# Head outputs to token rows: a 64-column weight block for the 64-token tile, and fixed PSUM banks

## The chip, the cores and the metric

One core of a Trainium2 chip runs the whole program. The metric is the device time of one execution in microseconds. The kernel before was run three times: 501.88, 502.3 and 503.22 us, median 502.3 us. Lower is better.

## The reference

Two batches, 8 heads, 576 tokens, head dimension 64. Queries and keys are rotated, then come softmax attention, the gathering of the heads into rows of 512 numbers a token (1152 tokens), a routed layer with 8 experts, of which each token takes one, and a last gated layer:

```python
scores = scale * np.matmul(q_rot, k_rot.transpose(0, 1, 3, 2))
attn = np.exp(scores - max) ; attn = attn / (sum + 1e-09)
x = (attn @ v).transpose(0, 2, 1, 3).reshape(B * S, H * D)        # token rows
logits = x @ w_gate + modality_bias[modality_id]                  # chooses the expert
out[mask] = gate_w[mask, None] * (np.maximum(x[mask] @ w1[e], 0) @ w2[e])
h = out @ w_in ; result = (h * np.tanh(softplus(h))) @ w_out
```

All in float32.

## The kernel before, in words

**Stages.** Attention (about 17 to 170 us), then expert tiles of 304 token rows with weights that are chosen at run time (to about 291 us), then the last gated layer. Products that need more than one pass of the tensor engine's number format are done with a high and a low part (`F32R` tiles named `..h` and `..l`); the transposes and the products that make token rows are plain float32.

**Attention by units.** 576 queries of a head fall into tiles of 128, 128, 64, 128, 128 (`QT`). The 64-query tile of two neighbouring heads is worked as one shared tile (`QMIX`, j = 2): rows 0 to 63 for the odd head, 64 to 127 for the even one. Each head has two units (`Unit`): hf = 0 with the tiles up to 320 queries, hf = 1 with the last two. A unit goes through these steps, each by its own function:

- `score` (PE, L963), `smax` (DVE, L973), `sexp` (ACT, L984): scores in PSUM, the negated row maximum, the exponentials. For the shared tile the scores of the odd head's queries take a 128-column and those of the even head's a 64-column weight operand.
- `tr` (PE, L997): exponentials are transposed, 128 or, for the last key block, 64 keys at a time, into a PSUM bank.
- `t_hi` (ACT, L1017) and `t_lo` (DVE, L1023): high and low part of the bank into SBUF. After `t_lo` the bank is free.
- `pv` (PE, L1038): the product with the values, accumulated in the bank `avp`, head dimension on the partitions (high part 0 to 63, low part 64 to 127), queries along the row; `f_evac` (ACT, L1047) copies it to `avt`.
- `f_mm` (PE, L1068): turns the head output round into token rows. The weight operand is a block of 128 columns of `avt` (128 queries), the moving operand `mov` has 72 columns: an identity that adds high and low part, and the head's 8 columns of the routing weights. A unit hf = 1 has two blocks; a unit hf = 0 has three, the third being the 64-query tile. For even heads the third block starts at column 256, its last 64 columns being a stretch of `avt` set to zero at the start; for odd heads it starts at column 0, and its last 64 columns are queries of the next tile. The three blocks lie side by side in one PSUM bank.
- `f_norm` (DVE, L1078): multiplies all 128 rows of the two or three blocks by the reciprocal sums and writes token rows `X`. Rows 64 to 127 of the 64-query tile's block are no token's, and no later step takes them as one.

**Banks.** Three PSUM banks `pt0` to `pt2` serve `tr`, `f_mm` and the routing's `counts` in turn. `bank` makes a new tile under the tag of the bank whose turn it is; the tile framework adds the waits on the readers of the tile that stood there before.

**Order.** `Plan` writes the order of all instructions of the stage ahead of time: a greedy list over PE, ACT, DVE, POOL and the SP queue. Each step has an assumed duration, dependences, resources that it takes and gives back (bank ring, exponentials, score banks) and a due time (`K`, 10 units a head). At each turn the step that can start earliest is issued; among those that can start at once the one due first. Some steps may go to one of two engines. An engine's clock in the plan goes on by the assumed duration. The routing of the first batch (L337 to L524), its scatters on POOL (L408) and the first expert tile's preparation are worked in as streams, once their conditions are met. The listing of `f_mm` (L1179) is `0.22 * len(u.cols)`, so 0.44 or 0.66.

**After attention.** Expert weights are loaded by the SP queue in chunks (`wraw`) as their buffers come free, after the routing table is in registers; the last layer's packed weights (`wr`) are loaded in between and unpacked on DVE.

Of the kernel before, what the change touches and what calls it, by code (L numbers as in the profile page):

```python
# [10 lines left out]
F32 = mybir.dt.float32  # L11
# [7 lines left out]
B, H, S, D = 2, 8, 576, 64  # L19
# [193 lines left out]
def moe_kernel(ctx: ExitStack, tc: tile.TileContext, aps, out):  # L213
# [596 lines left out]
    def attention(actx, hook):  # L810
# [5 lines left out]
        ps_t = actx.enter_context(tc.tile_pool(name="ps_t", bufs=1, space=PSUM))  # L816

        avp = ps_t.tile([128, 512], F32, tag="av", name="av")
        scp = [ps_s.tile([128, 2, 512], F32, tag=f"sc{z}", name=f"sc{z}") for z in range(2)]
        cur["rtile"] = scp[0][:, 1, NC2:512]  # L820
        spare = [0, 0.0, 0]
# [13 lines left out]
        mov = a_c.tile([128, H, XW], F32, name="mov")  # L835
# [10 lines left out]
                )  # L846

        def bank(name):
            return ps_t.tile([128, 512], F32, tag=f"pt{plan.at}", name=name)

        vraw, vhl, xin, ab, qk = {}, {}, {}, {}, {}
        sc, pexp, st, rs, pt, ph, pl, av, avsb, xo, nm = ({} for _ in range(11))
# [137 lines left out]
        def tr(n, hf, kts):  # L990
            kn = KT[kts[0]][1]
            pt[n, hf, kts] = t = bank(f"pt{n}_{hf}_{kts[0]}")
            o = 0
            for kt in kts:
                k0 = KT[kt][0]
                for j in U[n, hf].js:
                    nc.tensor.transpose(  # L997
                        out=t[:kn, o:o + 128], in_=pexp[n, j][:, k0:k0 + kn], identity=ident
                    )
                    o += 128  # L1000
# [63 lines left out]
        def f_mm(n, hf):  # L1064
            t = bank(f"xo{n}_{hf}")
            xo[n, hf] = t[:, :3 * XW].rearrange("p (a c) -> p a c", a=3)
            for i, c in enumerate(U[n, hf].cols):
                nc.tensor.matmul(  # L1068
                    xo[n, hf][:, i], lhsT=avsb[n, hf][:, c:c + 128], rhs=mov[:, n % H],
                    start=True, stop=True,  # L1070
                )

        def f_norm(n, hf):
# [20 lines left out]
        plan = Plan(  # L1094
            {"pe": 9.6, "act": 11.0, "dve": 11.8, "pool": 10.0, "sp": 7.0},
            {"sc": [0.0] * 2, "pexp": [0.0] * 5, "ph": [0.0] * 2, "pha": [0.0], "av": [0.0], "qs": [0.0, 8.6],
             "vhl": [0.0] * 2, "xs": [], "vraw": [11.9], "ab": [0.0], "avt0": [0.0],
             "avt1": [0.0], "st": [0.0] * 8},
            [0.0] * 3,
        )  # L1100
# [4 lines left out]
        def op(name, eng, dur, key, fn, *a, deps=(), line=None, **kw):  # L1105
            go = (lambda: fn(*a)) if isinstance(eng, str) else lambda: fn(*a, plan.eng)
            plan.op((name,) + a, eng, dur, key, go, deps=deps, line=line, **kw)

        for n in range(B * H):
            z = 10.0 * n  # L1110
# [20 lines left out]
        for q in range(4 * (B * H) // 2):  # L1131
            p, o = divmod(q, 4)
            n, hf = 2 * p + ORDER[o][0], ORDER[o][1]
            z = 20.0 * p
            if o == 0:
                tiles = groups = 0
            u = U[n, hf]
            for i, j in enumerate(u.js):
                k = tiles + i
                line = [("score",) + was] * bool(was)  # L1140
                op("score", "pe", 0.525 if j == QMIX else 0.485, z + K["sc"][k], score, n, j,
                   deps=[("stack", n)] + [("stack", n + 1)] * (j == QMIX) + line,
                   take=[("sc", (n, j))], give=[("qs", n)] * (j == QMIX or (n % 2 and j == 4)))
                op("max", "dve", 0.665, z + K["max"][k], smax, n, j, deps=[("score", n, j)])
                line = [("exp",) + e_was] * bool(was)
                op("exp", "act", 0.717, z + K["exp"][k], sexp, n, hf, i, j,
                   deps=[("max", n, j)] + line,
                   take=[("pexp", 0)] + ([("st", (n, hf))] if i == 0 else []),
                   give=[("sc", (n, j))])
                was, e_was = (n, j), (n, hf, i, j)  # L1150
            last = len(u.groups) - 1
            pair = "pha" if u.pair else "ph"
            for i, kts in enumerate(u.groups):
                m = len(kts)
                a = (n, hf, kts)
                k = groups + i
                prev = (n, hf, u.groups[i - 1])
                op("tr", "pe", 0.11 * m * len(u.js), z + K["tr"][k], tr, *a,
                   deps=[("exp", n, hf, x, j) for x, j in enumerate(u.js)],
                   take=[("ring", a)], give=[("pexp", 0)] * len(u.js) if i == last else [],  # L1160
                   line="tr")
                op("hi", "act", 0.05 + u.w * m / 1200.0, z + K["hi"][k], t_hi, *a,
                   deps=[("tr",) + a] + [("hi",) + prev] * (i > 0),
                   take=[(pair, a)] if i == 0 and o != 2 else [], line="hi")
                op("lo", "dve", 0.07 + u.w * m / 960.0, z + K["lo"][k], t_lo, *a,
                   deps=[("hi",) + a], give=[("ring", a)], line="lo")
                more = [("lo", n - 1, 0, (kt,)) for kt in kts] if o == 2 else []
                op("pv", "pe", u.nq * m / 2400.0 * (1 if i == last else 2), z + K["pv"][k], pv, *a,
                   deps=[("lo",) + a, ("vlo", n)] + [("pv",) + prev] * (i > 0) + more,
                   take=[("av", a)] if i == 0 else [], line="pv",  # L1170
                   give=([(pair, a)] * (o != 1) + [("vhl", n)] * (o % 2)) * (i == last))
            a = (n, hf)
            op("evac", "act", 0.05 + u.nq / 1200.0, z + K["evac"][o], f_evac, *a,
               deps=[("pv", n, hf, u.groups[-1])], take=[(f"avt{hf}", a)], give=[("av", a)])
            op("rec", "pool", 0.2 if o == 2 else 0.1, z + K["rec"][o], f_rec, *a,
               deps=[("exp", n, hf, len(u.js) - 1, u.js[-1])],
               give=[("st", a)] * ((1, 0, 2, 1)[o]))
            op("inv", "dve", 0.09, z + K["norm"][o] - 2.0, f_inv, *a, deps=[("rec",) + a])
            op("fmm", "pe", 0.22 * len(u.cols), z + K["fmm"][o], f_mm, *a, deps=[("evac",) + a],  # L1179
               take=[("ring", a)], give=[(f"avt{hf}", a)])  # L1180
            op("norm", "dve", 0.08 + 0.095 * len(u.cols), z + K["norm"][o], f_norm, *a,
               deps=[("fmm",) + a, ("inv",) + a], give=[("ring", a)])
            tiles += len(u.js)
            groups += len(u.groups)
        for i in range(14):
            op("zero", "sp", 0.5, 20.0 + 5.0 * i, setup_dma, i, deps=[("stack", 3 + i // 3)])
        op("bias", "pool", 2.5, 60.0, setup_bias)
        hook(plan, bank)
        plan.run()

# [83 lines left out]
    with ExitStack() as actx:  # L1274
        attention(actx, hook)
# [63 lines left out]
    with ExitStack() as mctx:  # L1339
# [87 lines left out]
        def pool(name, bufs, **kw):  # L1427
            return ectx.enter_context(
                tc.tile_pool(name=name, bufs=bufs, reuse_waits="tile", **kw)
            )  # L1430

        w2p, yp, gp, op = (
            pool(n, b) for n, b in (("w2p", 1), ("yp", 1), ("gp", 3), ("op", 5))
        )
# [129 lines left out]
        for q in range(nq):  # L1564
# [9 lines left out]
            for i in range(2):  # L1574
                u = LATE.get((nq - q, i), m + i)
# [6 lines left out]
            o = m + Q["o"]  # L1582
# [14 lines left out]
        for i, (q, t) in enumerate(TAIL):  # L1597
            w = 2 * nq + (0.6 if i < 5 else 4)
# [75 lines left out]
```

## Time and profile before

| | us |
|---|---|
| median of three runs | 502.3 |
| profiled execution | 500.64 |
| its span, first to last instruction | 498.9 |
| PE busy | 469.3 |
| DVE busy | 397.7 |
| POOL busy | 362.8 |
| ACT busy | 331.4 |

Busy time is the union of the instructions of an engine. Matmuls are pipelined and their ends are modelled, so overlapping ones count once, and a busy PE need not be at its peak. PEld is the engine's weight load, PEldq its queue's separate semaphore instructions. The chain of waits is followed back from the last instruction; its pieces give start and length in microseconds, the engine, the kernel line and the number of instructions. The granted TensorE clock was 0.999 of full speed over the whole span, 2.4 GHz.

### The profile page before, as it was taken

How to read it: one execution, taken by the hardware profiler on the slowest of the kernel's cores; microseconds unless marked ns; L12 is line 12 of the kernel's file. 1: busy time of each engine (PE TensorE's matmuls, PEld its weight loads, DVE VectorE, ACT ScalarE, POOL GpSimd, SP SyncE). 2: the span in 40 equal slices, each digit the busy share in tenths (PEclk: the TensorE clock that was granted, in tenths of full speed). 3: DMA queues.
4: the chain of work that ended last, by engine and by line, in shares of the span. 5: the costliest groups of instructions: out<-in, count | busy, mean ns of one | idle time of the engine just before them, and what ended most of it. 6: DMA issues, size and time to landing. Idle time of an engine off the chain costs nothing.

```text
span 498.9 us, 9097 instructions
## 1 busy us (share of the span) xinstructions
PE 469.3 (94%) x3152; PEld 436.9 (88%) x3152; DVE 397.7 (80%) x614; ACT 331.4 (66%) x750; POOL 362.8 (73%) x367
## 2 busy tenths in 40 slices
PE   0689999998999999999999999999999999999995
PEld 0589999998998798998989998899889989999994
DVE  5878989899788676663586879999999958777773
ACT  2378888777776845554465488665755878767763
POOL 4979999999970455765767567778777769966764
PEclk9999999999999999999999999999999999999999
DMA  7579995787654278895888630020100001100002
GB/s 220 131 180 218 242 232 169 186 211 190 161 157 166 84 224 333 324 313 211 284 301 315 235 107 0 2 85 11 76 0 1 1 1 62 44 1 1 3 1 84
DMA packets 24132, 69.43 MB, mean 139 GB/s; under 512 B 5522, under 2 KB 9810, under 8 KB 22034
## 3 DMA queue, kind: packets, MB, share of 16 engines
q1 hardware_dynamic: 21794, 63.16, 41.5%
q0 software_dynamic: 1456, 5.03, 2.5%
q10 hardware_dynamic: 832, 0.61, 0.5%
q8 instruction: 26, 0.43, 0.3%
q14 instruction: 24, 0.20, 0.1%
HBM read 49.08 MB, written 6.44 MB: 111 GB/s over the span
## 4 chain that ended last, share of the span: by engine, by line
PE 68%; DVE 15%; issue 5%; DMA 4%; ACT 4%; POOL 3%; POOLq 0%; SPq 0%; ACTq 0%; DVEq 0%
PE h L1471 15%; PE o L1528 14%; PE mm L695 13%; PE sc L963 8%; PE av L1038 7%; PE pt L997 7%; DVE ta L1493 6%; PE xo L1068 3%; DVE nm L973 2%; DMA wr<-in_wio_dram 1%; DMA tabs<-in_rope_dram 1%; DMA wraw(0, 1)_6_3129<-in_w_dram 1%; PE mm L661 1%; DVE pl L1023 1%; ACT pexp L984 1%
## 5 line engine op out<-in xcount | busy, mean ns | idle before, releaser
L1493 DVE RECIPROCAL ta<-ta 128x320 f32<-128x320 f32 (+1 forms) x64 | 124.7, 1949 | 22.4 <-ACT ta L1486 21.5
L1528 PE MATMUL o<-w2h,g 128*128 128x512 f32 x288 | 99.7, 395 | 0.1
L1451 POOL TENSOR_TENSOR w2l<-wc,w2h 128x512 fp32r<-128x512 f32 x64 | 89.2, 1416 | 7.1 <-DVE yl L1415 3.9
L1511 POOL TENSOR_TENSOR g<-ta,g 128x320 fp32r<-128x320 f32 (+1 forms) x63 | 52.9, 840 | 32.9 <-issue 14.7
L1471 PE MATMUL h<-yl,w2h 128*128 128x320 f32 (+1 forms) x256 | 75.8, 296 | 0.1
L1471 PE MATMUL h<-yh,w2h 128*128 128x320 f32 (+1 forms) x256 | 75.8, 296 | 0.0
L1471 PE MATMUL h<-yh,w2l 128*128 128x320 f32 (+1 forms) x256 | 75.7, 296 | 0.0
L963 PE MATMUL sc<-sk,sq 128*128 128x288 f32 (+1 forms) x320 | 58.3, 314 | 17.4 <-DVE sq L884 11.3
L984 ACT ACTIVATE pexp<-sc,nm 128x576 f32<-128x576 f32 x72 | 53.3, 740 | 23.1 <-DVE nm L973 17.6
L1528 PEld LDWEIGHTS o<-w2h,g 128*128 128x128 f32 x288 | 54.0, 188 | 10.7 <-POOL g L1511 0.7
L1017 ACT ACTIVATE ph<-pt 128x512 fp32r<-128x512 f32 (+2 forms) x112 | 54.5, 509 | 13.1 <-PE pt L997 12.5
L963 PEld LDWEIGHTS sc<-sk,sq 128*128 128x128 f32 (+1 forms) x320 | 46.4, 190 | 19.0 <-ACT sk L890 11.3
L973 DVE TENSOR_REDUCE nm<-sc 128x1 f32<-128x576 f32 x72 | 53.5, 752 | 11.4 <-PE sc L963 7.5
L997 PE MATMUL pt<-ident,pexp 128*128 128x128 f32 (+1 forms) x360 | 54.7, 277 | 2.3 <-DVE pl L1023 1.7
L1528 PE MATMUL o<-w2l,g 128*128 128x512 f32 x144 | 56.7, 394 | 0.0
L1023 DVE TENSOR_TENSOR pl<-pt,ph 128x512 fp32r<-128x512 f32 (+1 forms) x80 | 49.0, 630 | 3.9 <-ACT ph L1017 3.1
L1038 PE MATMUL av<-ph,vhl 128*128 128x256 f32 (+1 forms) x160 | 50.8, 333 | 1.0 <-POOL vhl L916 0.6
L1471 PEld LDWEIGHTS h<-yl,w2h 128*128 128x128 f32 x256 | 48.1, 188 | 2.9 <-DVE yl L1415 0.4
L1471 PEld LDWEIGHTS h<-yh,w2h 128*128 128x128 f32 x256 | 48.2, 188 | 2.7 <-DVE ta L1494 0.2
L1471 PEld LDWEIGHTS h<-yh,w2l 128*128 128x128 f32 x256 | 48.2, 188 | 0.0
L997 PEld LDWEIGHTS pt<-ident,pexp 128*128 128x128 f32 (+1 forms) x360 | 42.2, 137 | 5.1 <-issue 1.6
L1482 ACT ACTIVATE ta<-h 128x320 f32<-128x320 f32 (+1 forms) x64 | 25.7, 402 | 27.4 <-PE h L1471 22.2
(444 smaller groups left out, 1205.3 us busy)
## 6 DMA issues: line engine op xcount, KB each, us to landing
wr<-in_wio_dram SPq DMA_DIRECT2D x16, 1024.0 KB
xs<-in_qk_dram SPq DMA_DIRECT2D x15, 576.0 KB
sk<-ab SPq DMA_DIRECT2D x30, 288.0 KB
sq<-ab SPq DMA_DIRECT2D x30, 144.0 KB
vraw<-in_v_dram SPq DMA_DIRECT2D x16, 160.0 KB
scratch<-zero SPq DMA_DIRECT2D x12, 108.8 KB
xrow(0, 0)_2307<-scratch SPq DMA_DIRECT2D x2, 290.0 KB
xrow(0, 1)_2671<-scratch SPq DMA_DIRECT2D x2, 290.0 KB
```

Of the source, the lines that this page charges most:

```text
L695: nc.tensor.matmul(ps[:, :T], lhsT=w, rhs=m, start=(n == 0), stop=(n == 3 * len(pairs) - 1))
L963: nc.tensor.matmul(t[:m, hf, :NC2], lhsT=sq[:, c:c + m], rhs=sk[:, z, hf * NC2:(hf + 1) * NC2], start=(z == 0), stop=(z == 1),)
L973: nc.vector.tensor_reduce(out=nm[n, j], in_=sc[n, j][:, :, :NC2], axis=AX.XY, op=ALU.max, negate=True)
L984: nc.scalar.activation(out=pe, in_=sc.pop((n, j))[:, :, :NC2], func=AF.Exp, bias=nm.pop((n, j)), accum_out=st[n, hf][:, i:i + 1],)
L997: nc.tensor.transpose(out=t[:kn, o:o + 128], in_=pexp[n, j][:, k0:k0 + kn], identity=ident)
L1017: nc.scalar.activation(out=block(ph, n, hf, kts, slice(0, kn)), in_=psum(n, hf, kts, kn), func=AF.Copy)
L1023: nc.vector.tensor_tensor(out=block(pl, n, hf, kts, slice(0, 128)) if kn == 128 else block(ph, n, hf, kts, slice(64, 128)), in0=psum(n, hf ...
L1038: nc.tensor.matmul(av[n, hf][:, :u.nq], lhsT=vhl[n][:, kt].rearrange("p a d -> p (a d)"), rhs=src[:, kt, u.at:u.at + u.nq], start=(kt == 0 ...
L1451: nc.gpsimd.tensor_tensor(out=lo[:, cs], in0=w[:, cs], in1=hi[:, cs].bitcast(F32), op=ALU.subtract)
L1471: nc.tensor.matmul(ps[:, :w], lhsT=wt[:, c], rhs=m[g, i][:, c], start=(n == 0), stop=(n == 11))
L1493: nc.vector.reciprocal(out=ta, in_=ta)
L1528: nc.tensor.matmul(acc[g, t], lhsT=a[:, s], rhs=b, start=(f == 0 and z == 0), stop=(f == FC2 - 1 and z == 2),)
```

## The change

The third block of a three-block unit takes 64 columns of `avt` as its weight operand and writes rows 0 to 63 of its part of the bank; rows 64 to 127 there keep what was in the bank. The plan's duration for a three-block unit goes from 0.66 to 0.55, that of a two-block unit stays at 0.44. The three banks become three tiles, made once, which `bank` hands out in turn.

```diff
         avp = ps_t.tile([128, 512], F32, tag="av", name="av")
+        ptb = [ps_t.tile([128, 512], F32, tag=f"pt{z}", name=f"pt{z}") for z in range(3)]
...
         def bank(name):
-            return ps_t.tile([128, 512], F32, tag=f"pt{plan.at}", name=name)
+            return ptb[plan.at]
...
             for i, c in enumerate(U[n, hf].cols):
+                w = 64 if i == 2 else 128
                 nc.tensor.matmul(
-                    xo[n, hf][:, i], lhsT=avsb[n, hf][:, c:c + 128], rhs=mov[:, n % H],
+                    xo[n, hf][:w, i], lhsT=avsb[n, hf][:, c:c + w], rhs=mov[:, n % H],
                     start=True, stop=True,
                 )
...
-            op("fmm", "pe", 0.22 * len(u.cols), z + K["fmm"][o], f_mm, *a, deps=[("evac",) + a],
+            op("fmm", "pe", 0.11 * (2 * len(u.cols) - (len(u.cols) > 2)), z + K["fmm"][o], f_mm, *a, deps=[("evac",) + a],
```

## Rows read from the trace of the kernel before

**Rows 1.** The page: span, PE's busy time, shares of the chain by engine
```profile
span 498.9 us, 9097 instructions
...
PE 469.3 (94%) x3152; PEld 436.9 (88%) x3152; DVE 397.7 (80%) x614; ACT 331.4 (66%) x750; POOL 362.8 (73%) x367
...
PE 68%; DVE 15%; issue 5%; DMA 4%; ACT 4%; POOL 3%; POOLq 0%; SPq 0%; ACTq 0%; DVEq 0%
```

**Rows 2.** Windows: length, busy PE, PEld, DVE, ACT, POOL, clock, DMA share, GB/s
```profile
46.40:63.92 17.52, 17.52 (x143) 17.20 (x142) 15.50 (x31) 14.61 (x37) 16.60 (x19) 1.00 0.93 235
63.92:81.34 17.42, 17.42 (x143) 17.14 (x142) 15.64 (x32) 14.60 (x37) 15.98 (x27) 1.00 0.76 195
...
98.78:102.26 3.48, 3.06 (x24) 2.46 (x22) 3.32 (x8) 2.40 (x8) 3.23 (x4) 1.00 0.96 217
...
114.70:124.40 9.70, 8.42 (x66) 7.36 (x65) 9.43 (x19) 7.76 (x20) 9.12 (x10) 1.00 0.86 210
...
144.90:153.20 8.30, 6.77 (x53) 6.33 (x53) 7.33 (x22) 5.52 (x14) 3.96 (x8) 1.00 0.27 93
153.20:170.60 17.40, 16.16 (x123) 14.72 (x123) 12.40 (x27) 14.93 (x36) 5.44 (x6) 1.00 0.39 130
...
191.00:291.70 100.70, 99.79 (x696) 96.14 (x696) 65.20 (x117) 55.90 (x98) 64.85 (x28) 1.00 0.75 274
```

**Rows 3.** The chain of waits in the attention stage: start, length, what, count
```profile
36.60 0.62 PE xo L1068 x6
...
68.26 0.40 PE xo L1068 x4
...
74.63 1.05 PE sc L963 x8
...
77.27 1.06 PE sc L963 x8
...
164.93 0.62 PE xo L1068 x6
```

**Rows 4.** Line L1068: count, ns minimum/median/maximum, first and last start, form
```profile
L1068 PEld LDWEIGHTS xo<-mov,avt x160: 186/192/192, 25.4 to 170.3; 128*128 128x128 f32 x160
L1068 PE MATMUL xo<-mov,avt x160: 223/275/330, 25.4 to 170.3; 128*128 128x72 f32 x160
L1068 PEldq EVENT_SEMAPHORE  x19: 51/51/51, 24.5 to 166.0; - x19
```

**Rows 5.** PE's timeline at the start of a three-block unit: start, length
```profile
71.43 0.34 PE L1068 MATMUL xo<-mov,avt 128*128 128x72 f32 x2
```

**Rows 6.** Weight loads by form, 46.4 to 98.7 us: count, busy us, mean ns
```profile
L963 PEld LDWEIGHTS sc<-sk,sq 128*128 128x128 f32 x108 | 15.5, 189 | 0.0
L997 PEld LDWEIGHTS pt<-ident,pexp 128*128 128x128 f32 x108 | 13.0, 142 | 0.0
...
L997 PEld LDWEIGHTS pt<-ident,pexp 128*64 128x64 f32 x27 | 2.9, 110 | 0.3
L963 PEld LDWEIGHTS sc<-sk,sq 128*64 128x64 f32 x12 | 1.6, 135 | 0.0
```

**Rows 7.** PE's matmuls by form, 77.11 to 78.1 us, a shared score tile
```profile
L963 PE MATMUL sc<-sk,sq 128*64 128x288 f32 x4 | 0.9, 295 | 0.0
L963 PE MATMUL sc<-sk,sq 128*128 128x288 f32 x4 | 0.8, 294 | 0.0
```

**Rows 8.** Line L997: separate semaphore instructions on PE's queue
```profile
L997 PEldq EVENT_SEMAPHORE  x24: 51/51/51, 38.4 to 163.1; - x24
```

**Rows 9.** PE's waits, 17 to 171 us: total us, times, longest
```profile
PE pt L997 <- DVE pl L1023: 1.7, 3, 0.9
```

**Rows 10.** The chain of waits in the expert tiles
```profile
212.96 6.66 DMA wraw(0, 1)_6_3129<-in_w_dram
...
242.13 7.26 DMA wr<-in_wio_dram
```

## The prediction

> **What bounds the kernel now.** Read the page first, then the windows, then the chain of waits. The profiled execution took 500.64 us, its span is 498.9 us, so 1.74 us lie around the span; it is 1.66 us under the median of the runs shown, 502.3 us. On the page PE is busy for 94% of the span and holds 68% of the chain [rows 1]. The edits all lie in the attention stage, roughly 17 to 170 us, so its windows decide. From 46 us on the kernel repeats itself, one pair of heads every 17.4 to 17.5 us, and PE is busy in every microsecond of it, while POOL has 15.98 to 16.60 us of work in a pair, DVE 15.50 to 15.64 and ACT 14.6 [rows 2]. The chain agrees: between 26 and 98.8 us its pieces are PE pieces that follow one another without a gap [rows 3]. There a microsecond saved on PE is a microsecond saved, as long as POOL, the next engine, keeps 0.8 us of slack a pair. In three later places the chain leaves PE: for the routing arithmetic on DVE from 98.8 us, for the scatters on POOL from 144.9 us, and at the stage's end [rows 2]. After 170 us no instruction of the change runs.
>
> **The narrower block.** Of the 80 products that turn head outputs into token rows, 16 change: the last one of each unit with three blocks (hf = 0), one a head. Each product is two weight loads and two matmuls, 160 of each in all [rows 4]. On the chain a unit of two blocks costs 0.40 us in four matmuls, one of three 0.62 us in six [rows 3]: 0.22 us for the third block, 0.11 us a matmul. Is that the load or the stream of 72 columns? A load of 128 columns takes 192 ns, and the first two matmuls of a group, whose loads were done early, last 0.34 us together where one lasts 0.27 us, so they start 0.07 us apart; in the body they start 0.11 us apart [rows 4, 5]. The body waits for loads, and the stream alone would allow 0.07 us. How much a load of half the columns saves can be read from the scores and the transposes, which have both widths: 189 against 135 ns in the scores, 142 against 110 ns in the transposes [rows 6], so 54 or 32 ns a load. Two loads a unit: 0.06 to 0.11 us. The stream's floor of 0.07 us, itself read from rounded rows, leaves about 2 x 0.04 to 2 x 0.05. I take 0.10 us a unit, nearest to the scores' rows, since there as here nothing but the width differs; the ends kept are 0.06 and 0.11.
>
> Of the 16 three-block units 13 stand on the chain as pieces of six (the first at 36.60, the last at 164.93 us); the other three run where DVE, POOL or ACT releases the chain [rows 3]. 13 x 0.10 = 1.3 us; by the ends 13 x 0.06 = 0.8 and, if all 16 pay, 16 x 0.11 = 1.8 us.
>
> Does the chip charge for going from a 128-column to a 64-column load and back? The score of the shared tile alternates both: four matmuls of either form, in 1.06 us, where two plain tiles shortly before it, eight of one form, take 1.05 us [rows 3, 7]. Its changes of width cost 0.01 us together, within what the pieces scatter. I put the change of width at nothing.
>
> The Trainium skill speaks against this ("TensorEngine Tiling (Array Packing)", Key Properties): a change of tiling mode, not only of tile, drains the engine. If a 64-column load is such a mode, every unit would pay for two drains and the sum would turn to a loss; the rival on draining below prices it from rows. The shared score tile [rows 3, 7] shows no such pause, so here I side with the trace.
>
> **The fixed banks.** Three tiles made once replace a new tile at each use. The same three banks, the same rotation, and the same rule for their reuse in the plan: a bank comes back after the DVE subtraction or the normalising multiply that reads it last. What can differ is how the waits are spelled. Now 24 separate semaphore instructions of 51 ns stand before transposes on PE's queue and 19 before head outputs [rows 4, 8]. If all 43 on PE vanished and had been exposed, 43 x 0.051 = 2.2 us would go; if each of the 144 uses of a bank (112 groups of transposes, 32 units) got one, exposed, 101 x 0.051 = 5.2 us would come. But PE is busy without a break where these stand [rows 2], so they run ahead of the matmuls in progress. I take zero. The cover is PE's queue being full; where PE waits anyway they would cost their 51 ns.
>
> The lower half of the third block now keeps what an earlier transpose left in the bank. The normalising multiply still reads all 128 rows, its shape is unchanged, and the old data's writer is long done: nothing.
>
> **The planner's price.** The listing of a three-block unit falls from 0.66 to 0.55 in the plan, two-block units stay at 0.44. This moves no instruction by itself, but the plan is a greedy list: each later start on PE shifts by 0.11, and where two candidates are close, the order on all five queues changes. The real pieces cost 0.62 and by my sum will cost 0.52, so the plan stays about as true as it was. What a new order costs can't be read off: PE's waits in the stage bound it. PE lost nothing in the pairs; it idled 0.4 us at the routing, 1.3 us from 114.7, 1.5 us from 144.9 and 1.2 us from 153.2 us [rows 2]. A better order could win these 4.4 us at most; a worse one has no such floor. Single waits of PE's transposes on DVE are 1.7 us in three, up to 0.9 us [rows 9]. I take zero as the middle.
>
> **What passes on to the end.** From 170 to 291 us come the expert tiles. Their chain crosses two loads, 6.66 us at 212.96 and 7.26 us at 242.13 us [rows 10], and DMA is at 0.75 of its engines' time from 191 to 291.7 us [rows 2]. These loads are issued as buffers come free, and the first wait for the routing table, which comes after 12 of the 13 units; so they start earlier by about what attention saves, and I let all of it through. From 291.8 us the last stage runs by itself. What is late next in attention is still PE: 0.2 us a pair is a quarter of POOL's slack.
>
> Sum: 500.64 - 1.3 = 499.3 us for a profiled run; on the median 502.3 - 1.3 = 501.0 us.
>
> **Rivals.**
> - A new order with a wait in every pair (slower). Place: PE's transposes, held by the DVE subtraction that frees their bank. DVE has only 1.8 us of slack in a pair, and the bank ring has three places. The mean of the three waits there is now 0.57 us [rows 9]; one in each of seven pairs is 4.0 us, less the 1.3 us saved: 502.3 + 2.7 = 505.0 us. It beats the gain from 0.19 us a pair on. For it: the cycle of the pairs was free of idle time on PE, so a change of order there can only lose. Against it: PE's work is 1.8 us or more a pair above DVE's and ACT's.
> - A new order that closes gaps. Half of the 4.4 us of PE's idle time after 98.8 us goes as well: 502.3 - 1.3 - 2.2 = 498.8 us. For it: those stretches are irregular, and DVE or POOL end last in them.
> - The gain stays inside. Either the load is no narrower in time than the stream that follows it (against it [rows 6]), or the loads of the expert tiles start where they did and the two DMA waits grow by what attention gave: 502.3 us. Against it: the loads follow the table.
> - Draining. Each of 16 units changes width twice. A drain would leave the 0.27 us of a matmul instead of the 0.11 us from start to start [rows 3 to 5]: 32 x 0.16 = 5.1 us more, less 1.3: 506.1 us. Against it: the shared score tile [rows 3, 7].
>
> **How the numbers follow.** What can be told from no change here is about 0.3%, 1.5 us: faster is under 500.8, slower over 503.8 us. My forecast, the order kept in substance and 0.8 to 1.8 us saved, 45%, own range 500.5 to 501.5 us; it lies on the border, so I split it evenly between faster and same. The closing of gaps 18%, faster. The wait in every pair 22%, a quarter of it too small to tell. The gain kept inside 10%, same. Draining 5%, slower. Faster 0.225 + 0.18 = 0.40; same 0.225 + 0.055 + 0.10 = 0.38; slower 0.165 + 0.05 = 0.22. Range 498.5 to 504.5 us: it takes in closed gaps below, and above most of the price of a new order; the drains and the worst orders are left out.
>
> **What would show it.** The 64-column loads of the head outputs at about 135 ns against 192, 32 of the 160; a three-block piece on the chain at 0.52 us instead of 0.62; the pair's period 17.2 us with PE still busy throughout; semaphore instructions on PE near 43; the first expert tile's and the last stage's starts earlier by the same 1.3 us. Wrong would be: a period above 17.4 us with PE waiting for DVE in the pairs, a pause before or after the narrow block, or an earlier end of attention followed by longer waits for loads. If the order of the queues differs much, the sum above is only one term of what is measured.

## The result, and the profile after

The changed kernel is slower. In the first comparison its median was 504.31 us over ten runs against 501.51 us over ten of the kernel before; the ratio on record is 1.0069 with a 95% interval of 1.0047 to 1.0091. (The two medians alone give 1.0056: the ratios on record, here and below, are not quotients of medians.) A second comparison gave 1.0107 (1.0072 to 1.0142). The prediction said 501.0 us, in a range of 498.5 to 504.5, with faster as the likeliest sign; on its base of 502.3 us the first ratio makes 505.8 us.

The profiled run took 505.58 us. Its page (span; busy time, share and instructions of each engine; the granted clock of TensorE in 40 slices, in tenths; shares of the chain), against [rows 1]:

```profile
span 503.8 us, 9143 instructions
...
PE 475.9 (94%) x3152; PEld 441.5 (88%) x3152; DVE 396.0 (79%) x614; ACT 332.1 (66%) x750; POOL 362.2 (72%) x367
...
PEclk9969999999999999999999999999999999999999
...
PE 77%; DVE 7%; DMA 5%; POOL 4%; issue 3%; ACT 3%; SPq 1%; POOLq 0%; ACTq 0%; DVEq 0%
```

PE has the same 3152 matmuls and is busy 6.6 us longer. Part of that is no work of the change: the 6 in the clock row is a stretch of 10.2 us from 23.9 us at half the clock (1.2 GHz, a granted clock of 0.50), while PE waited there for a load. It is taken up at the end; it makes the two spans unfit for a direct comparison. The stretches that repeat are fit for one. Windows of three pairs, each cut from the start of a three-block unit to the same unit of the next pair (length, then busy time and instructions of PE, PEld, DVE, ACT, POOL, then clock, DMA share, GB/s), against the first two lines of [rows 2]:

```profile
38.69:56.66 17.97, 17.88 (x144) 17.25 (x143) 15.48 (x33) 14.55 (x38) 16.59 (x16) 1.00 0.84 204
56.66:74.62 17.96, 17.87 (x143) 17.24 (x143) 15.45 (x32) 14.59 (x38) 16.74 (x18) 1.00 0.92 240
74.62:92.58 17.96, 17.87 (x143) 17.24 (x143) 15.51 (x32) 14.58 (x37) 16.03 (x27) 1.00 0.64 166
```

A pair takes 17.96 us where it took 17.52 and 17.42, at the full clock. PE is still the engine that is busy nearly throughout: it has 0.4 us more to do in a pair, and 0.09 us of idle time that it did not have. The other engines' work is what it was. So the loss is on PE itself, in a stage where the change takes columns away from it.

The chain of waits over one pair says where (start, length, what, count), against [rows 3]:

```profile
74.62 0.67 PE pt L1070 x6
75.28 0.59 PE pt L998 x4
...
79.35 0.67 PE pt L1070 x6
80.02 1.15 PE av L1039 x8
81.17 1.06 PE sc L964 x8
82.23 0.23 PE pt L998 x2
82.46 0.02 issue
82.48 0.38 ACT ph L1018
82.86 0.28 ACT avt L1048
83.14 0.04 issue
83.18 0.67 PE pt L1070 x4
...
89.25 0.40 PE pt L1070 x4
```

Line L1070 is the head-output product (L1068 before; its bank is now named `pt`). The six matmuls of a three-block unit take 0.67 us where they took 0.62. The transposes that follow take 0.59 us for four, where four took 0.44: 0.15 us more, in work that the change does not touch. The same unit on the chain of the kernel before:

```profile
71.59 0.62 PE xo L1068 x6
72.21 0.44 PE pt L997 x4
```

That makes 0.05 + 0.15 = 0.20 us a unit, two units a pair. And once a pair the chain leaves PE, through a copy of `avt` on ACT that a two-block unit waits for (82.46 to 83.18 us); in the kernel before the same unit followed PE work without a gap.

The loads of that line, all forms, against [rows 4] (count, ns minimum/median/maximum, first and last start, forms):

```profile
L1070 PEld LDWEIGHTS pt<-mov,avt x160: 133/190/193, 22.2 to 174.8; 128*128 128x128 f32 x128, 128*64 128x64 f32 x32
L1070 PE MATMUL pt<-mov,avt x160: 223/275/331, 22.2 to 174.9; 128*128 128x72 f32 x128, 128*64 128x72 f32 x32
L1070 PEldq EVENT_SEMAPHORE  x18: 51/51/51, 21.4 to 170.2; - x18
```

32 loads are 64 columns wide and last from 133 ns. The load did become shorter, as forecast. The weight loads' timeline of the unit at 74.62 us shows what came with it (start, length):

```profile
74.33 0.54 PEld L1070 LDWEIGHTS pt<-mov,avt 128*128 128x128 f32 x4
...
74.94 0.19 PEld L1070 LDWEIGHTS pt<-mov,avt 128*64 128x64 f32 x2
75.21 0.31 PEld L998 LDWEIGHTS pt<-ident,pexp 128*128 128x128 f32 x3
```

Four wide loads end at 74.87 us, the first narrow one starts at 74.94: 0.07 us in which nothing is loaded, on an engine whose loads otherwise overlap. The narrow ones end at 75.13, and the next wide load starts at 75.21: 0.08 us again. Over the whole kernel the group of these narrow loads, by form, has 1.2 us of idle time in front of it (columns: busy us, mean ns, idle us just before):

```profile
L1070 PEld LDWEIGHTS pt<-mov,avt 128*64 128x64 f32 x32 | 3.1, 135 | 1.2
```

1.2 us over 16 units is 0.075 us each: every unit pauses. From start to start in the trace: before the change the six matmuls of a three-block unit were 62, 110, 112, 111 and 112 ns apart, the first transpose behind them came after another 112 and the second after 109, together 728 ns. Now the same steps are 62, 110, 112, **205** and 113, then **157** and **165**, together 924 ns. In the other three-block unit of a pair, which a value product follows, the like steps went from 792 to 985 ns. A unit costs PE 0.19 to 0.20 us more; 16 units, 3.1 us.

The rest of the span, for the terms that the prediction named. From the first three-block unit to the first expert tile's product there are 136.4 us after (136.3 in the second profile of this kernel), where the two profiles of the kernel before have 134.0 and 134.1. From there to the last stage 120.4 and 121.2, where before 119.6 and 120.0. The last stage takes 208.5 to 208.9 us in every profile but one (210.0 us, the one-pass product below).

### The profile page after: what moved, and what is told of

Its sections match the earlier page's. It is cut to its first block, busy times and chain, and to the rows that moved or that the text cites. A ratio compares the mean times of both kernels' runs of the same rounds, so it can differ in the third digit from the quotient of the medians.

```text
span 503.8 us, 9143 instructions
## 1 busy us (share of the span) xinstructions
PE 475.9 (94%) x3152; PEld 441.5 (88%) x3152; DVE 396.0 (79%) x614; ACT 332.1 (66%) x750; POOL 362.2 (72%) x367
## 4 chain that ended last, share of the span: by engine, by line
PE 77%; DVE 7%; DMA 5%; POOL 4%; issue 3%; ACT 3%; SPq 1%; POOLq 0%; ACTq 0%; DVEq 0%
PE h L1473 20%; PE o L1530 19%; PE mm L695 12%; PE sc L964 7%; PE av L1039 7%; PE pt L998 6%; PE pt L1070 3%; DVE nm L974 2%; DMA xs<-in_qk_dram 2%; DMA wr<-in_wio_dram 1%; DVE pl L1024 1%; PE mm L661 1%; DMA wraw(0, 1)_6_2987<-in_w_dram 1%; DMA sk<-ab 1%; POOL xs L905 1%
## 5 line engine op out<-in xcount | busy, mean ns | idle before, releaser
L1453 POOL TENSOR_TENSOR w2l<-wc,w2h 128x512 fp32r<-128x512 f32 x64 | 90.3, 1431 | 7.1 <-DVE yl L1417 3.9
L964 PE MATMUL sc<-sk,sq 128*128 128x288 f32 (+1 forms) x320 | 61.0, 323 | 15.6 <-ACT sk L891 9.7
L964 PEld LDWEIGHTS sc<-sk,sq 128*128 128x128 f32 (+1 forms) x320 | 48.6, 198 | 17.4 <-ACT sk L891 9.7
L1530 PEld LDWEIGHTS o<-w2h,g 128*128 128x128 f32 x288 | 54.1, 188 | 10.2
L998 PE MATMUL pt<-ident,pexp 128*128 128x128 f32 (+1 forms) x360 | 56.6, 284 | 2.6 <-DVE X L1080 1.6
```

Source lines behind the costliest of these rows:

```text
L964: nc.tensor.matmul(t[:m, hf, :NC2], lhsT=sq[:, c:c + m], rhs=sk[:, z, hf * NC2:(hf + 1) * NC2], start=(z == 0), stop=(z == 1),)
L998: nc.tensor.transpose(out=t[:kn, o:o + 128], in_=pexp[n, j][:, k0:k0 + kn], identity=ident)
L1453: nc.gpsimd.tensor_tensor(out=lo[:, cs], in0=w[:, cs], in1=hi[:, cs].bitcast(F32), op=ALU.subtract)
L1530: nc.tensor.matmul(acc[g, t], lhsT=a[:, s], rhs=b, start=(f == 0 and z == 0), stop=(f == FC2 - 1 and z == 2),)
```

## The experiments

The theory after this result: the change from 128-column to 64-column loads and back pauses PE, about 0.3 us a unit gross (0.20 net of a saving of 0.10), and that is the loss. Rivals: the new order that the plan's listing makes; the waits of the fixed banks; a price of the narrow product itself, whatever stands before it. All times are given as ratios to the kernel before, run in between on the same chip.

### The banks alone

```diff
-                w = 64 if i == 2 else 128
+                w = 128
...
-            op("fmm", "pe", 0.11 * (2 * len(u.cols) - (len(u.cols) > 2)), ...
+            op("fmm", "pe", 0.22 * len(u.cols), ...
```

> The three fixed banks alone: the third block stays 128 columns wide, the plan's listing stays 0.22 a block, so the order of all queues is that of the kernel before. Theory A (the narrow block itself costs: PE pauses before and after a 64-column load in plain float32, about 0.20 us a unit, 16 units, 3.1 us): no change, within 1 us of before, pair period 17.4 to 17.5 us. Theory B (the new listing's order costs): no change as well. Theory C (the fixed banks add waits that are paid): slower by 2 us or more, with longer waits of the transposes.

1.0013 (0.9987 to 1.0038), 502.64 us. The order of the instructions is that of the kernel before, and its three-block units stand on the chain at 0.62 us. What the fixed tiles did to the waits (semaphore instructions of the transposes on PE, and of the high parts on ACT):

```profile
L998 PEldq EVENT_SEMAPHORE  x6: 51/51/51, 39.0 to 164.0; - x6
...
L1018 ACTq EVENT_SEMAPHORE  x62: 17/17/17, 31.3 to 166.9; - x62
```

On PE 24 [rows 8] became 6; on ACT 62 of 17 ns appeared where there were none, about 1.1 us of ACT's time spread over the stage. No loss can be told from this comparison, and none of the size looked for. The pairs took 17.43, 18.58 and 17.40 us. The second is longer than was expected; there POOL's preparation of the next head's queries and keys stands on the chain (POOL has 17.68 us of work in it).

### The banks and the new listing

```diff
-                w = 64 if i == 2 else 128
+                w = 128
```

> Fixed banks and the new listing, third block 128 columns wide: every queue in the order of the changed kernel, without the narrow block. Theory A: little, between 0 and 1 us slower, pair period 17.5 to 17.6 us, because in the changed kernel's pair of 17.97 us two narrow blocks take 0.39 of the 0.52 us added. Theory B: most of the 3.5 us, pair period about 17.9 us. Theory C: as with the banks alone.

1.0029 (0.9999 to 1.0058), 502.97 us. Here the order is exactly the changed kernel's, with blocks of full width. A pair takes 17.56 us, with PE at 17.47 of them:

```profile
57.20:74.76 17.56, 17.47 (x143) 17.14 (x142) 15.39 (x31) 14.49 (x37) 16.10 (x19) 1.00 0.92 235
```

The same 0.09 us of idle time as in the changed kernel, and the chain has the same step through ACT once a pair:

```profile
80.47 0.02 issue
80.49 0.38 ACT ph L1018
80.87 0.28 ACT avt L1048
81.15 0.04 issue
81.19 0.67 PE pt L1070 x4
```

So the new order costs about 0.1 us in each regular pair: it puts four value products ahead of a score, and the two-block unit then comes before its copy is done. Over the whole of attention it costs more, 0.6 to 1.0 us: 135.0 us here, 134.4 and 134.0 in the two profiles with the banks alone. Between this run and the one before, 0.16% is within what either interval leaves open. The ratio here is less than half of the changed kernel's 0.69%, but the two intervals overlap, so the totals of these runs do not separate them.

### The banks and the narrow block, in the old order

```diff
-            op("fmm", "pe", 0.11 * (2 * len(u.cols) - (len(u.cols) > 2)), ...
+            op("fmm", "pe", 0.22 * len(u.cols), ...
```

> Fixed banks and the 64-column third block, listing as before, so the order of the kernel before. Theory A: slower by 2.5 to 3.5 us; a unit of three blocks and what follows it on PE 0.20 us longer than before, pair period about 17.85 us. Theory B: faster by about 1.3 us, as the prediction had it.

1.0049 (1.0024 to 1.0074), 503.17 us: slower than before, with the order of before. (With the banks alone it was 1.0013 and, further down, 1.0029; the totals alone do not separate these runs either.) Its pairs, and the chain around one unit:

```profile
35.15:52.98 17.83, 17.83 (x144) 17.25 (x143) 15.73 (x33) 14.61 (x38) 16.91 (x16) 1.00 0.92 228
52.98:70.78 17.80, 17.80 (x143) 17.22 (x143) 15.54 (x32) 14.60 (x37) 16.71 (x18) 1.00 0.92 236
```

```profile
88.62 0.67 PE pt L1070 x6
89.28 0.59 PE pt L998 x4
```

PE is busy in every microsecond of the pair, the step through ACT is gone, and the period is 17.82: the 17.47 of before plus 0.35, near the 2 x 0.196 that two units lose. The narrow block by itself lengthens the pair, and the order adds the other 0.1. Attention takes 135.5 us here, 1.2 to 1.5 us more than with the banks alone.

### Other widths, in the old order

```diff
-                w = 64 if i == 2 else 128
+                w = 96 if i == 2 else 128     (the first run)
+                w = 72 if i == 2 else 128     (the second run)
```

with the listing of 0.22 a block.

> As the run before, but the third block takes 96 columns (rows 64 to 95 of it are no token's). Order of the kernel before. Theory A1 (the pause belongs to the operand of 64 columns, a layout of the array of its own): no pause, the two loads are some 27 ns shorter each, 0 to 0.9 us faster than before, pair period 17.3 to 17.5 us. Theory A2 (in plain float32 any change of width makes PE pause): slower by 2.5 to 3.5 us, as with 64 columns. Theory B: faster by some 0.6 us.

> Third block of 72 columns, listing as before, fixed banks; order of the kernel before. If the pause belongs to an operand of 64 columns or fewer (A1): no pause, each of the two loads about 47 ns shorter than at 128 columns, a three-block unit some 0.09 us shorter on PE; at most 16 x 0.09 = 1.5 us, less where POOL and the loads of the next head release the chain, as they did with 96 columns: between 1.5 us faster and 0.5 us slower than before. If any width that is no multiple of 32 is laid out as 64 columns (rival): pauses as with 64, 2 us slower.

96 columns: 1.0011 (0.9984 to 1.0039), 501.92 us. 72 columns: 1.0001 (0.9971 to 1.003), 501.26 us. Neither differs from the kernel before. The groups of their narrow loads, first with 96, then with 72 columns:

```profile
L1070 PEld LDWEIGHTS pt<-mov,avt 128*96 128x96 f32 x32 | 4.0, 165 | 0.0
```

```profile
L1070 PEld LDWEIGHTS pt<-mov,avt 128*72 128x72 f32 x32 | 3.4, 145 | 0.0
```

The chain at one unit with 72 columns, and the window of one pair:

```profile
72.13 0.53 PE pt L1070 x6
```

```profile
72.13:89.37 17.24, 17.24 (x143) 16.96 (x143) 15.54 (x32) 14.64 (x37) 16.03 (x27) 1.00 0.66 171
```

No idle time in front of them where 64 columns have 1.2 us. With 72 columns the steps from start to start, counted as above, are 61, 110, 112, 112, 65, 65 and 109 ns, together 634: a narrow load saves 47 ns, the unit stands on the chain at 0.53 us instead of 0.62, and where PE sets the pair the period is 17.24 us. That is the gain that the prediction worked out (0.10 us a unit, 17.2 us a pair). Attention as a whole takes 132.9 us with 72 columns, 1.1 us less than in the kernel before; the total does not show it, and in this profile the expert tiles take 122.3 us, 2.3 to 2.7 us more than in the two profiles of the kernel before. Not every pair gains: in the pair before this one and in most of the run with 96 columns, POOL's preparation of the next head's queries and keys stands on the chain (with 96 columns also a transfer that sets a scratch to zero), and the pair is held at 17.7 to 17.8 us. The slack that the prediction gave POOL (0.8 us a pair) was a mean of busy time and not a promise on each pair.

### The narrow block as a one-pass product

```diff
-    avt = [[a_c.tile([128, 384], F32, name=f"avt{f}") for f in range(2)]]
+    avt = [[a_c.tile([128, 384], F32R, name=f"avt{f}") for f in range(2)]]
+    movr = a_c.tile([128, H, XW], F32R, name="movr")      (a copy of mov)
...
-    xo[n, hf][:w, i], lhsT=avsb[n, hf][:, c:c + w], rhs=mov[:, n % H],
+    xo[n, hf][:w, i], lhsT=a if i == 2 else a.bitcast(F32),
+    rhs=(movr if i == 2 else mov)[:, n % H],
```

The third block then loses the low bits of its operands. Old listing.

> The 64-column block with both operands in the rounded one-pass format (F32R, so its product loses the low bits; one load and one matmul instead of two of each), other blocks in plain float32, listing as before. Theory A (the pause is one of plain float32 with 64 columns): the matmul starts 0.11 us after the one ahead of it, as the scores' 64-column matmuls do after 128-column ones, and the next follows without a gap. Rival D (the pause comes from writing 64 rows of a bank beside 128-row blocks, or from any 64-column load after a plain float32 one): 0.20 us before the block and a gap of some 0.08 us of the weight load after it, as in the changed kernel.

504.45 us, a single run, whose first unit came 3 us late; only its stretches are used. The weight loads of one unit, one load for the third block instead of two:

```profile
74.37 0.54 PEld L1072 LDWEIGHTS pt<-mov,avt 128*128 128x128 f32 x4
74.83 0.14 PEld L1072 LDWEIGHTS pt<-movr,avt 128*64 128x64 f32 x1
74.91 0.42 PEld L999 LDWEIGHTS pt<-ident,pexp 128*128 128x128 f32 x4
```

The 64-column load starts at 74.83 us, before the wide ones end at 74.91, and the next wide load at 74.91, before it ends. Same width, same place, same neighbours, and no pause. The steps are 78 ns to the narrow matmul (110 was expected), 67 to the first transpose and 155 to the second. The last two make 222 ns, and the two steps behind a unit of full-width blocks 112 + 109: nothing is lost. So it is not the 64 columns alone. It is 64 columns in a product of plain float32, which the chip works as two loads and two matmuls (160 of each for 80 products, [rows 4]). Whether the number type or the two passes make the difference was not separated.

### The narrow product twice

```diff
-                nc.tensor.matmul(
+                for _ in range(2 if i == 2 else 1):
+                    nc.tensor.matmul(
```

A product is repeated into the same place; old listing.

> The 64-column product of each three-block unit issued twice in a row, in plain float32 (the second writes the same rows again). Theory A in the form 'pause at the change of layout': starts 0.205, then 0.11 three times, then the pause at the end, so the second product costs 0.22 to 0.23 us. Rival (each plain 64-column product waits until the one before has drained): 0.205 again at its start, the second product costs 0.31 us or more.

503.65 us, a single run. Its loads, and two of its pairs:

```profile
L1071 PEld LDWEIGHTS pt<-mov,avt 128*64 128x64 f32 x64 | 5.1, 136 | 1.2
```

```profile
36.00:54.07 18.07, 18.07 (x148) 17.49 (x147) 15.73 (x33) 14.67 (x38) 16.78 (x16) 1.00 0.86 208
54.07:72.12 18.05, 18.05 (x147) 17.47 (x147) 15.55 (x32) 14.66 (x38) 16.43 (x18) 1.00 0.93 239
```

Twice the narrow loads, and the same 1.2 us of idle time in front of them. Steps: 205 ns to the first narrow matmul, 113, 63 and 62 among the four narrow ones, then 157 and 166. The second product costs 0.125 us, less than a wide one (0.22) and less than either theory had expected. The pair is 0.24 us longer than with one product (18.06 against 17.82), which is 2 x 0.125. The pause belongs to going in and coming out, once a unit, and not to the narrow product.

### The kernel before, profiled again

> The kernel before, profiled once more, to see what differs between executions of one program: the pair period should be 17.4 to 17.5 us again with PE busy throughout; the first 30 us, where the loads land in another order each time, may differ by 1 to 2 us, and the granted clock may fall to half there.

500.82 us, a single run. Its stretches are in the account above; it tells how far two profiles of one program lie apart: 134.0 and 134.1 us in attention, 119.6 and 120.0 us in the expert tiles, with the first unit at the same time within 0.05 us. Its pairs took 17.48, 17.51 and 17.72 us, the last above what was expected.

### The changed kernel, 64 against 72 columns

The first run is the changed kernel again. The second differs from it by one number:

```diff
-                w = 64 if i == 2 else 128
+                w = 72 if i == 2 else 128
```

> The changed kernel once more, as the neighbour of the next two on one chip: 1.005 to 1.009 of the kernel before, pair period 17.96 us.

> The changed kernel with 72 columns in place of 64 in the third block: the same order on every queue, the same banks, nothing of the layout of 64 columns. Theory A: the pair period falls from 17.96 to 17.38 us (two pauses of 0.19 go and two savings of 0.095 come), the whole 2 to 3.5 us faster than the changed kernel, so 0.999 to 1.003 of the kernel before; what is left is the new order's. Theory B (the order is the main loss): 1.004 or more, period 17.8 us or more.

64 columns: 1.0107 (1.0072 to 1.0142), a median of 506.14 us over six runs; the ratio is above what was expected. 72 columns: 1.0009 (0.9981 to 1.0038), 501.82 us. Eight more columns, on the same chip, with the same order, banks and plan, take back 4.3 us of the medians, and the two intervals do not meet. So the width of 64 costs time: the two programs differ in nothing else. With 72 columns no load of the group waits, in this order too:

```profile
L1070 PEld LDWEIGHTS pt<-mov,avt 128*72 128x72 f32 x32 | 3.4, 145 | 0.0
```

From 64 to 72 columns a unit goes from 924 to 634 ns, 0.29 us; 16 units are 4.6 us of PE's time. That this is near the 4.3 us does not show that all of it reached the end. The two profiled executions, at 502.50 and 502.15 us, are 0.35 us apart, and attention is 1.3 us shorter with 72 columns (135.1 against 136.3 us). Its pairs take 17.44, 17.48 and 18.42 us (17.38 was expected), the third held by POOL's preparation of the next head and the transfer of its keys. The six runs with 64 columns lie between 502.50 and 507.58 us; where the rest of the 4.3 us lies, these profiles do not show.

### The banks alone, again

> The fixed banks alone again, since the first comparison (1.0013, 0.9987 to 1.0038) leaves open whether their 62 added semaphore instructions on ACT's queue cost anything. If they do, about 1 us: 1.001 to 1.004 again; if not, 0.998 to 1.001.

1.0029 (1.0001 to 1.0058), 502.30 us, the same program as the first experiment. The two together say 0.1 to 0.3%, about 1 us, at the edge of what can be told. In attention this run has 134.0 us, as the kernel before. In the expert tiles all eleven profiles with fixed banks have more than the two without, some of them by little: 120.2 to 125.1 us against 119.6 and 120.0. On the chain of this run POOL comes to a weight chunk late, by pieces of which the kernel before has none at this place:

```profile
202.13 7.21 DMA wraw(0, 1)_2_2865<-in_w_dram
...
210.56 0.13 POOL wlo(0, 1)_2_2908 L603
210.69 1.41 issue
...
212.14 0.77 issue
212.91 2.42 POOL wlo(0, 1)_3_2949 L603
```

Why a rewrite of the attention's tiles should delay POOL 40 us later was not tried. The programs differ in instructions on ACT and PE (9142 against 9097), and the queue that brings instructions has one or two packets more; whether that is the cause stays open, and so does whether the cost is real.

**The stretches side by side.** Attention is counted from the first three-block unit to the first product of the expert tiles, the expert tiles from there to the last stage. Two numbers are two profiles of one program.

| order | third block | attention, us | expert tiles, us |
|---|---|---|---|
| old, kernel before | 128 | 134.0, 134.1 | 119.6, 120.0 |
| old, fixed banks | 128 | 134.4, 134.0 | 122.7, 120.7 |
| old, fixed banks | 64 | 135.5 | 125.1 |
| old, fixed banks | 64, one pass | 133.1 | 120.2 |
| old, fixed banks | 64, twice | 137.0 | 120.2 |
| old, fixed banks | 96 | 133.9 | 121.8 |
| old, fixed banks | 72 | 132.9 | 122.3 |
| new, fixed banks | 128 | 135.0 | 121.2 |
| new, fixed banks (the changed kernel) | 64 | 136.4, 136.3 | 120.4, 121.2 |
| new, fixed banks | 72 | 135.1 | 120.8 |

Two profiles of one program agree to 0.4 us in attention, and only to 2 us in the expert tiles. So, against full width, the 64 columns cost 1.4 us of attention in the new order and 1.2 to 1.5 in the old, and the new order costs 0.6 to 1.0 us.

No version beats both kernels by more than can be told: the best, 72 columns in the old order, is level with the kernel before. Narrow blocks without the fixed banks would leave rows of the bank unwritten that the normalising multiply reads; it was not tried.

## Why the prediction was wrong

**The step that failed is "I put the change of width at nothing".** The term was 0; it measured 0.29 us a unit gross (64 against 72 columns), 0.196 net of the saving, and where the sum had 1.3 us saved, attention lost 1.4 us to the narrow block. The prediction asked the right question and answered it from the wrong row. The shared score tile [rows 3, 7] does alternate 128 and 64 columns without a pause, and still does: in the changed kernel its eight matmuls take 1.06 us (81.17 us on the chain above). But the score's operands are the high and low parts, one load and one matmul to a product; the head output is plain float32, two loads and two matmuls. The row that decides would have been one with the same number of passes and a 64-column load, and the trace of before had none. The narrow transposes [rows 6], plain float32 too, are single instructions. An operation that the trace does not show should have been bounded from both sides; this one was bounded for its saving (0.06 to 0.11) and not for its change.

The Trainium skill ("TensorEngine Tiling (Array Packing)", Key Properties) has the rule that a change of tiling mode drains the engine. The trace agrees for the two-pass product with 64 columns (0.07 and 0.08 us without a load, once in and once out, and not between two narrow products), and shows no pause for the one-pass product of the same shape. With 72 and 96 columns there is none either. Which of these products change the mode no trace tells, so that the pause is such a drain stays argued. The prediction weighed that rule and sided with the row that did not bear on it.

**The rival on draining, given 5%, is nearest to what happened.** It put a drain in place of each change, 32 x 0.16 = 5.1 us gross; the runs show 16 x 0.29 = 4.6 on PE. Its time, 506.1 us on a median of 502.3, is a ratio of 1.0076; measured 1.0069 (1.0047 to 1.0091). Its condition, a pause at each change, was right and its price was right to a tenth, although the trace shows less than it assumed: 93 ns going in, 45 and 56 ns coming out. That its total came so near is in part luck: it had no term for the new order, and it let all 16 units pay. Of PE's 16 x 0.196 = 3.1 us net only 1.2 to 1.5 us reach attention. In the old order the first four pairs are 0.35 to 0.4 us longer each and the three after them, where the chain often stands on other engines, are not; so fewer units paid than the 13 that the prediction counted on the chain.

**The saving itself was right.** 0.10 us a unit was forecast from the scores' rows; 72 columns show 0.094, with a pair at 17.24 us where the text had 17.2, and 1.1 us of attention in the old order where the sum had 1.3. In the new order attention shows nothing of it (135.1 against 135.0 us). In the total it was worth nothing measurable: some pairs are held by POOL as soon as PE gains, and the expert tiles were longer, for a reason that was not found. "A quarter of POOL's slack" was too kind to POOL.

**The plan's price: too low as well.** Zero was the middle; the order did change, from 44 us on, and costs 0.1 us a regular pair through the copy of `avt` on ACT, not through the DVE subtraction that the rival on waits named, and 0.6 to 1.0 us over attention. It cannot be told in the total (1.0029, 0.9999 to 1.0058).

**The fixed banks: nearly right.** Of 43 semaphore instructions on PE 24 are left (6 + 18), and none of it shows in attention (134.4 and 134.0 us). That 62 new ones would stand on ACT was not seen; the cost, if there is one, is about 1 us and comes later, in the expert tiles.

**What passes on.** The loads of the expert tiles did shift with the end of attention, and the loss went through: the expert tiles are no shorter for it (120.4 and 121.2 us).

**Two readings of the rows.** The chain is not all PE between 26 and 98.8 us: at 27.20 us the row maximum on DVE (0.77 us) and at 28.00 us the exponentials on ACT (0.84 us) stand on it, before the regular pairs begin. And the 0.40 us of a two-block unit is one of two values on the chain, others stand at 0.61 us; the third block's 0.22 us holds all the same, by the steps of 111 and 112 ns. Neither changes the sum.

The account of the first comparison, from the stretches: attention +2.3 us (some 1.4 from the narrow block, 0.6 to 1.0 from the new order), expert tiles +0.4 to +1.7 us, last stage 0; 2.7 to 4.0 us, where the ratio says 0.0069 x 501.5 = 3.5 us and the medians 2.8 us. What lengthened the expert tiles stays open.

## What to carry to other kernels

A shorter instruction is not a cheaper one if it differs in shape from its neighbours: before narrowing an operand, find a row in the trace with the same data type, the same number of passes and the same width, and look at what starts after it, not at its own duration. Here a few more columns (72 for 64) kept the whole saving of a unit and lost its whole cost. A piece on the chain is not yet a piece that pays: measure a stage from end to end before multiplying by the count. And when the busiest engine has 0.8 us of slack over the next one in a mean pair, expect the next one to take what you save in the pairs where its work bunches.

## What the runs showed of the hardware

- A plain float32 product with a weight operand of 64 columns between wider ones: 0.07 us without a load before it and 0.08 us after, 0.29 us a unit in all against 72 columns. With 72 or 96 columns, or as a one-pass product of 64: no pause.
- Matmuls of these plain float32 head-output products (72 moving columns), one behind the other, start 111 ns apart with 128 weight columns, 85 with 96, 65 with 72, and those of a repeated 64-column product 62 to 63 ns apart. The transposes (plain float32, single instructions, 128 moving columns) start 109 ns apart with 128 and with 64 weight columns, and 108 to 113 ns apart where the width goes from 64 to 128: no pause.
- One program starts differently from run to run. The first three-block unit came at 38.5 us in one profile of the changed kernel and at 34.7 in the other. In the first, PE waited for a load that landed at 24.6 us, and its clock stood at half from 23.9 us on; in the second it did not fall. These two windows show it (clock in the third column from the right):

```profile
23.90:34.10 10.20, 8.67 (x36) 8.10 (x37) 4.63 (x8) 4.35 (x10) 6.97 (x8) 0.50 0.82 235
```

```profile
20.00:34.00 14.00, 10.79 (x77) 9.67 (x78) 9.29 (x18) 8.86 (x24) 11.78 (x15) 1.00 0.89 230
```

The mean clock of the ten runs of the changed kernel in the first comparison is 0.993, and that of the kernel before in the later ones 0.993 to 0.994. So this is scatter, some 4 us of it, and the reason why differences of 1 us were read from stretches and from medians of many runs. In the second comparison the six runs of the changed kernel have 0.990 against 0.994, so a part of its 1.0107 may be this scatter; the runs with 72 columns beside it have 0.991.
